# Moving masking and weight scaling between GpSimd and ScalarE in a top-k attention and channel-mixing kernel

## The chip, the cores and the metric

The kernel runs on one core of a Trainium2 chip. The metric is the time of one execution on the device in microseconds, as the median of several runs. The core has five engines that run side by side, each through its own list of instructions in order: TensorE (PE) for matrix products, VectorE (DVE), ScalarE (ACT), GpSimd (POOL) and SyncE (SP), which here only issues DMA transfers. They wait for each other through semaphores.

## The reference

Inputs are q, k and v of shape (8 batches, 8 heads, 576 rows, 64), float32, and the parameters U (576 x 32), V (32 x 576), w_ch1 (512 x 2048) and w_ch2 (2048 x 512). These four are float64, since they are float32 arrays multiplied by a float64 scalar. The kernel sees them as pairs of 32-bit words, low and high.

```python
scores = scale * np.matmul(q, k.transpose(0, 1, 3, 2))
kth = np.partition(scores, -32, axis=-1)[..., -32:-31]
scores = np.where(scores >= kth, scores, -1e9)
attn = softmax(scores)                    # over the last axis
x = concat_heads(np.matmul(attn, v))      # (8, 576, 512)
u = x + (x.T @ U @ V).T                   # per batch
out = u + np.maximum(u @ w_ch1, 0.0) @ w_ch2
```

So each row of 576 scores keeps its 32 largest values. The rest get no weight.

## The kernel before, in words

**Tiles and steps.** The work goes by head pairs g (32 of them, four per batch) and, within a pair, by row tiles t: four of 128 rows for both heads, and a tail t = 4 in which the 64 last rows of both heads share one tile. A list of steps holds them in order. In the first batch (g below 4) each tile is a step, 20 in all; later the tail shares the step of t = 3, so that a pair has four steps. The main loop goes over steps n and writes out by hand, per step, in which order the engines get their instructions. Because each engine works in order, that text order is the schedule.

**Finding the 32nd largest.** `front` is a generator, advanced by `next(here)` and `next(last)` at chosen places of a step. For each lane (one head's 128 x 576 scores) DVE finds the eight largest (L507, MAX8), replaces them by a very small number (L520) and finds the next eight (L525), four rounds in all. From the second batch on (`blocked`), scores are folded first: the larger of each two (L434) and the sum less the larger (L432, L435 on POOL) make halves that the rounds then search (L486, L488).

**Masking and weighing.** `ways` says how a lane is masked. A "gap" lane: ACT scales the 32nd value (L551), writes to E how far each score lies below it, times a huge factor (L554), and POOL subtracts that from the scores (L555, two operands). A "pooled" lane: POOL compares and multiplies (L530, one operand and a value per partition) and adds the outcome (L531, two operands). An "early" lane is masked on DVE (L534). In the first batch lane 1 is pooled and lane 0 a gap, apart from the last tile and the last tail of the batch; later all are gaps. Then ACT takes the exponential and its sum (`weigh`, L439). The gap lanes of step n - 1 are masked at the start of step n (`next(last)`), the pooled ones at the end of their own step.

**Turning and multiplying.** PE turns the weights (L617, L622), ACT copies them out (L618, L623), and PE multiplies by v (`values`, L691, L694). From pair 6 on DVE turns them in blocks (L581) with a trip through DRAM instead. `mixed` builds u for a batch, and `mlp` makes its two big products (L816, L834), which `fill` scatters over later steps as filler for PE. `mlp` of batch b can begin only when the attention of batch b is done. The last batch uses another product scheme (`closing`, L910).

**The parameters.** 36 pieces, most of them 128 x 512, are turned from float64 words to float32. One call of `next_params(1)` does three things in this order. It finishes the waiting ACT passes and joins the piece that was split at the call before (`f64_join`: a shift on DVE, L188, and two additions on POOL, L189 and L191). It splits the piece that was loaded at the call before (`f64_parts`: it queues three ACT passes, L176 scaling the high words into the destination, L177 from a byte of the low words, L180 the sign of the high words, written in place). It issues the load of a new piece (L154, SP, three buffers). `fill` also pops one queued pass each time. In the first batch a step has a call after the first round for t = 0, 1, 2 and one after the third for t = 0, 1, 3. In the second batch the calls stand before `fill` after the first round (not for g = 4, t = 3) and near the end of the step, after loads and turned keys.

**The start.** For the first pair `prep` turns queries on PE and copies them with ACT (L321, L323), then the 64 last rows of both (L313, L316), then the keys, copied by DVE. `scores` makes two PSUM tiles. For the first tile DVE copies the first one (L390) and ACT the second in two instructions (L391, L392).

The passages that the steps of the prediction lean on most:

```python
for c, chunk, *_ in gaps:
    gap = attn.tile([P, S], F32, tag="E", name="E")
    nc.scalar.activation(gap, chunk, AF.Relu, bias=least[:, c : c + 1], scale=-WIDEN)
    nc.gpsimd.tensor_tensor(chunk, chunk, gap, ALU.subtract)
```

Of the kernel before, what the change touches and what calls it, by code (L numbers as in the profile page):

```python
# [8 lines left out]
F32 = mybir.dt.float32  # L9
U8 = mybir.dt.uint8  # L10
U32 = mybir.dt.uint32
AF = mybir.ActivationFunctionType
# [14 lines left out]
def kernel(  # L27
# [94 lines left out]

    nudge = const.tile([P, 1], F32, name="nudge")
    nc.vector.memset(nudge, TINY)
    eps = const.tile([P, 1], F32, name="eps")
    nc.vector.memset(eps, 1e-9)

# [10 lines left out]
        return slice(h * D, (h + 1) * D)  # L138

    SLAB = 512  # L140
    spare = []


# [13 lines left out]
    def f64_parts(raw, out):  # L157

        n, w = raw.shape[0], raw.shape[-1] // 2
        d = "p f" if len(raw.shape) == 3 else "p"
        low, hi = (raw.rearrange(f"{d} (w two) -> {d} w two", two=2)[..., i] for i in range(2))
        low8 = raw.bitcast(U8).rearrange(f"{d} (w eight) -> {d} w eight", eight=8)[..., 3]
        if out is None:
            if not spare:

                uT = mlpp.tile([P, NC, S], F32, tag="uT", name="uT")
                words = uT.rearrange("p c n -> p (c n)").bitcast(U32)  # L170
                spare.extend(words[:, i * SLAB : (i + 1) * SLAB] for i in range(NT))
            out = spare.pop()[0:n, 0:w]
        bits = out.bitcast(U32)
        lows, his = low.bitcast(F32), hi.bitcast(F32)
        passes.extend((
            lambda: nc.scalar.activation(bits.bitcast(F32), his, AF.Copy, scale=RESCALE),  # L176
            lambda: nc.scalar.activation(  # L177
                lows, low8, AF.Identity, bias=four[0:n], scale=-(1 + 2.0**-10) * 2.0**-26
            ),
            lambda: nc.scalar.activation(his, his, AF.Sign, bias=nudge[0:n]),  # L180
        ))
        return hi, bits, low
# [118 lines left out]
    def prep(g):  # L301

        qkT = attn.tile([P, 2, S], F32, tag="qkT", name="qkT")
        qkTs[g] = qkT
        if blocked(g):
            nc.vector.transpose(qkT.rearrange("p i n -> p (i n)"), raw.pop(g))
            yield
            return
        tiles, ends = raw.pop(g)
        for i in (0, 2, 1) if g == 0 else (0, 1, 2):  # L310
            if i == 2:
                tp = ps_t.tile([P, 2, TAIL], F32, tag="tp", name="tp")
                nc.tensor.transpose(  # L313
                    tp.rearrange("p i n -> p (i n)"), ends.rearrange("p h d -> p (h d)"), ident
                )
                nc.scalar.copy(qkT[:, :, MAIN:S], tp)  # L316
                yield
                continue
            tp = ps_t.tile([P, NT, P], F32, tag="tp", name="tp")
            for c in range(NT):  # L320
                nc.tensor.transpose(tp[:, c, :], tiles[i][:, c].rearrange("p h d -> p (h d)"), ident)  # L321
            copy = nc.vector.tensor_copy if g == 0 and i else nc.scalar.copy
            copy(qkT[:, i, 0:MAIN], tp.rearrange("p t n -> p (t n)"))  # L323
            yield

    def scores(g, t, tail=False):
# [61 lines left out]
        last = S2[:, MAIN : MAIN + 2 * TAIL].rearrange("p (h n) -> p h n", h=2)  # L388
        copy = nc.vector.tensor_copy if g + t == 0 else nc.scalar.copy
        copy(main[:, :, 0:HALF], scs[0][:, :, 0:HALF])  # L390
        nc.scalar.copy(main[:, :, HALF:MAIN], scs[1][:, :, 0 : MAIN - HALF])  # L391
        nc.scalar.copy(last, scs[1][:, :, MAIN - HALF : HALF])  # L392
        if tail:
            tail_copies(g, scs, third)

# [45 lines left out]
    def ways(g, t):  # L441

        if (g, t) == (NPAIR - 1, NT - 1):
            return (0,), (), (1,)
        if (g, t) == (NPAIR - 1, NT):
            return (0,), (), ()
        if t == NT:
            return (), (), (0,)
        return ((), (1,), (0,)) if g < NPAIR else ((), (), (1, 0))

    def eased(g, t):
        return bool(ways(g, t)[2])

    def front(tiles):

# [4 lines left out]
        for g, t in tiles:  # L460
            if t == 0:
                dens[g] = small.tile([P, 2 * NT + 1], F32, tag="den", name="den", bufs=3)
            S2, den = S2s.pop((g, t)), dens[g]
            early, pooled, gaps = ways(g, t)
            n = S2.shape[1]
            fold_of = folds.pop((g, t), None)
            for c in (1, 0) if n == 2 else (0,):
                slot = c if n == 2 or len(tiles) == 1 else 2
                spot = CH * c + t if g >= NPAIR else 2 * t + c
                lanes.append((  # L470
                    slot,
                    S2[:, c],
                    den[:, spot : spot + 1],
                    [a[:, c] for a in fold_of] if fold_of else None,
                    "early" if c in early else "pooled" if c in pooled else "gap" if c in gaps else "",
                ))
        W = len(lanes)
        first = small.tile([P, 3, 8], F32, tag="first", name="first", bufs=3)
# [30 lines left out]
        for i in range(1, TOPK // 8):  # L509
            if i == 1:  # L510
                nc.scalar.mul(nmax[:, 0:W], first[:, 0:W, 0], -SCALE)
                Es = {}
                for c, chunk, _, _, way in lanes:
                    if way == "early":
                        Es[c] = attn.tile([P, S], F32, tag="E", name="E")
                        weigh(chunk, Es[c], nmax[:, c : c + 1])
            for c in order:

                nxt = places.pop(c, curs[c])
                nc.vector.match_replace(nxt, ms[c], curs[c], NEG)  # L520
                curs[c] = nxt
            m8 = small.tile([P, 3, 8], F32, tag="m8", name="m8", bufs=4)
            for c in order:
                ms[c] = m8[:, c]
                nc.vector.max(ms[c], curs[c])  # L525
            yield
        for c, chunk, total, _, way in lanes:
            if way == "pooled":
                gap = attn.tile([P, S], F32, tag="E", name="E")
                nc.gpsimd.tensor_scalar(gap, chunk, ms[c][:, 7:8], NEG, ALU.is_lt, ALU.mult)  # L530
                nc.gpsimd.tensor_tensor(chunk, chunk, gap, ALU.add)  # L531
        for c, chunk, total, _, way in lanes:
            if way == "early":
                nc.vector.scalar_tensor_tensor(  # L534
# [23 lines left out]
        if len(gaps) > 1:  # L558
            c, chunk, total, *_ = rest.pop(0)
            weigh(chunk, chunk, nmax[:, c : c + 1], total)  # L560
            yield
        for c, chunk, total, *_ in rest:
            weigh(chunk, chunk, nmax[:, c : c + 1], total)
        if t == NT and g != NPAIR - 1:
# [623 lines left out]
    for n in range(STEPS + 2):  # L1188
# [89 lines left out]
        for tile_ in tiles(n + 1):  # L1278
            if tile_[1] < NT:
                scores(*tile_, len(tiles(n + 1)) > 1)  # L1280
            fold(*tile_)
        turn()
        fill()
        turn()
# [7 lines left out]
        if n < STEPS and n - 2 >= ALONE and len(tiles(n - 2)) > 1:  # L1292
            scale(steps[n - 2][0][0])
        next(here, None)
        border = g == NPAIR and t == NT - 1
        if not border:
            next_params(1)
        fill()
        if n >= STEPS:
            if n == STEPS:  # L1300
# [3 lines left out]
        next(here, None)  # L1304
        for tile_ in tiles(n + 1):
            split(*tile_)
        fill()
        next(here, None)
        for tile_ in tiles(n - 1):
# [7 lines left out]
                coming = loading(g + 2) if g + 2 < NP else iter(())  # L1317
            next(coming, None)
        next(ready, None)
        if t != 0 or g == NPAIR + 1:  # L1320
            next_params(1)
        next(here, None)
        fill()
        fill()
# [35 lines left out]
```

## Time and profile before

| What | us |
|---|---|
| Median of 3 runs (1663.66 to 1663.92) | 1663.71 |
| The profiled execution's own time | 1662.32 |
| Its span | 1660.2 |
| Busy: PE, DVE, ACT, POOL | 1555.9, 1547.4, 995.1, 1009.4 |
| L555 on POOL, 243 times, mean | 1.419 |
| L530 on POOL, 15 times, mean in 20 to 230 us | 2.222 |
| L188 on DVE at 128 x 512, shortest, median, longest up to 340 us | 0.380, 0.408, 1.378 |

The profile is of one execution. A line of a timeline gives the start and the length in us, the engine, the line of the code, the operation, what is written from what, and in brackets the idle time of the engine before it and what ended it. In the slices, the span is cut into 40 equal parts (41.5 us each) and a digit gives the busy tenths of a part. The chain of waits follows the work back from the end: each piece of time goes to the instruction that the next one had to wait for. PE's ends are modelled, so a busy PE need not be at its peak.

### The profile page before, as it was taken

Reading aid. Unit: us, or ns where it says so; the run is one execution under the profiler, and the core shown is the slowest. Engines: PE = TensorE matmul, PEld = TensorE weight load, DVE = VectorE, ACT = ScalarE, POOL = GpSimd, SP = SyncE. Lnnn points to the kernel's source line nnn. Section 1 sums busy time; section 2 is a strip of 40 time slices with the busy share of each in tenths; the row PEclk is TensorE's granted clock in tenths of the full one; section 3 lists DMA queues with packets and bytes.
Section 4 is the critical chain, followed back from the end, with each engine's and each line's share of the span. In section 5 each row is a group of like instructions: output and inputs, shape, how many; then the busy total and the mean of one; then the engine's idle time right before and its main releaser. Section 6 shows DMA issues by size and latency. Waiting matters only on the chain.

```text
span 1660.2 us, 30248 instructions
## 1 busy us (share of the span) xinstructions
PE 1555.9 (94%) x9638; PEld 1183.2 (71%) x9638; DVE 1547.4 (93%) x4393; ACT 995.1 (60%) x2475; POOL 1009.4 (61%) x881
## 2 busy tenths in 40 slices
PE   4566698999899999999999999999999999999999
PEld 2444466777677887778777887778777887777776
DVE  7999998999999999999999999999999999994452
ACT  4888778665655666566665666565665656563320
POOL 4787669766656565656656565666666566663620
PEclk7777899999999999999999999999999999999999
DMA  3323223255555555554555565555555555543001
GB/s 88 90 83 92 69 83 86 63 128 133 131 131 130 140 148 138 127 142 130 130 128 137 133 154 133 131 139 133 139 122 142 127 146 135 141 126 97 10 1 29
DMA packets 280399, 189.42 MB, mean 114 GB/s; under 512 B 174288, under 2 KB 261168, under 8 KB 280240
## 3 DMA queue, kind: packets, MB, share of 16 engines
q1 hardware_dynamic: 259728, 117.62, 30.9%
q10 hardware_dynamic: 20512, 69.87, 13.6%
q8 instruction: 76, 1.25, 0.3%
q14 instruction: 83, 0.68, 0.1%
HBM read 116.49 MB, written 70.91 MB: 113 GB/s over the span
## 4 chain that ended last, share of the span: by engine, by line
PE 66%; DVE 25%; DMA 4%; SPq 1%; issue 1%; ACT 1%; POOL 1%; DVEq 0%; ACTq 0%; POOLq 0%
PE mm L834 21%; PE mm L816 19%; DVE m L525 8%; DVE upper L520 7%; PE sc L336 6%; PE O L694 5%; PE mm L910 3%; DVE first L507 3%; PE tp L910 2%; PE sc L910 2%; PE sc L368 2%; DMA PT<-away 2%; PE up L766 1%; DVE y L581 1%; DVE upper L488 1%; DVE place L520 1%
## 5 line engine op out<-in xcount | busy, mean ns | idle before, releaser
L834 PE MATMUL mm<-hT,w 128*128 128x320 f32 (+1 forms) x1792 | 462.1, 407 | 0.0
L816 PE MATMUL mm<-uT,w 128*128 128x320 f32 (+1 forms) x1792 | 459.8, 409 | 1.2 <-ACT hT L829 1.0
L555 POOL TENSOR_TENSOR Ssb<-Ssb,E 128x576 f32<-128x576 f32 x243 | 340.0, 1419 | 185.4 <-ACT E L554 185.2
L816 PEld LDWEIGHTS mm<-uT,w 128*128 128x128 f32 x1792 | 334.1, 190 | 100.7 <-issue 10.6
L834 PEld LDWEIGHTS mm<-hT,w 128*128 128x128 f32 x1792 | 332.0, 190 | 93.0 <-issue 10.2
L525 DVE MAX8 m<-upper 128x8 f32<-128x304 f32 (+1 forms) x774 | 362.5, 509 | 0.7
L520 DVE MATCH_REPLACE8 upper<-m,upper 128x304 f32<-128x304 f32 (+1 forms) x516 | 256.6, 504 | 0.0
L435 POOL TENSOR_TENSOR lower<-lower,upper 128x576 uint32<-128x576 uint32 x108 | 152.5, 1412 | 141.7 <-DVE upper L434 137.2
L432 POOL TENSOR_TENSOR lower<-Ssb 128x576 uint32<-128x576 uint32 x108 | 152.4, 1411 | 116.3 <-ACT Ssb L381 65.9
L439 ACT ACTIVATE Ssb<-Ssb,nmax 128x576 f32<-128x576 f32 x258 | 201.8, 784 | 28.8 <-POOL Ssb L531 10.3
L336 PE MATMUL sc<-qkT 64*128 64x288 f32 (+1 forms) x1056 | 176.9, 457 | 9.1 <-ACT Ssb L390 8.2
L554 ACT ACTIVATE E<-Ssb,least 128x576 f32<-128x576 f32 x243 | 176.3, 769 | 4.2
L488 DVE MAX8 upper<-lower 128x8 f32<-128x288 f32 x432 | 171.8, 438 | 2.3 <-POOL lower L435 2.3
L381 ACT COPY Ssb<-sc 128x576 f32<-128x576 f32 x216 | 127.7, 643 | 66.8 <-PE sc L336 66.3
L829 ACT ACTIVATE hT<-mm 128x320 f32<-128x320 f32 (+1 forms) x224 | 91.9, 411 | 107.3 <-PE mm L816 102.2
L581 DVE STREAM_TRANSPOSE y<-Ssb 128x512 f32<-128x512 f32 (+1 forms) x312 | 153.9, 544 | 0.0
L694 PE MATMUL O<-PT,va 128*64 128x128 f32 x2048 | 144.0, 284 | 0.0
L336 PEld LDWEIGHTS sc<-qkT 64*128 64x128 f32 (+1 forms) x1056 | 95.2, 196 | 49.2 <-issue 17.0
L694 PEld LDWEIGHTS O<-PT,va 128*64 128x64 f32 x2048 | 112.7, 140 | 16.2 <-issue 1.6
L520 DVE MATCH_REPLACE8 upper<-first,upper 128x304 f32<-128x304 f32 x216 | 97.5, 458 | 0.0
L486 DVE MATCH_REPLACE8 lower<-upper,lower 128x288 f32<-128x288 f32 x216 | 93.9, 442 | 0.0
L507 DVE MAX8 first<-upper 128x8 f32<-128x304 f32 x216 | 90.1, 458 | 0.0
(266 smaller groups left out, 2208.4 us busy)
## 6 DMA issues: line engine op xcount, KB each, us to landing
away<-y SPq DMA_DIRECT2D x416, 144.0 KB
PT<-away ACTq DMA_DIRECT2D x104, 576.0 KB
raw<-in_moe_w_ch_dram SPq DMA_DIRECT2D x32, 512.0 KB
va<-in_v_dram SPq DMA_DIRECT2D x64, 128.0 KB
scale<-rd ACTq DMA_DIRECT2D x56, 144.0 KB
out_dram<-ob SPq DMA_DIRECT2D x59, 128.0 KB
ld<-in_q_dram SPq DMA_DIRECT2D x108, 64.0 KB
ld<-in_k_dram SPq DMA_DIRECT2D x108, 64.0 KB
```

Of the source, the lines that this page charges most:

```text
L336: nc.tensor.matmul(out, lhsT=qkT[half(h), 0, cols(t)], rhs=qkT[half(h), 1, lo:hi], start=True, stop=True,)
L435: nc.gpsimd.tensor_tensor(bottom, bottom, top.bitcast(U32), ALU.subtract)
L439: nc.scalar.activation(E, chunk, AF.Exp, bias=nmax, scale=SCALE, accum_out=total)
L488: nc.vector.max(spot, lower)
L520: nc.vector.match_replace(nxt, ms[c], curs[c], NEG)
L525: nc.vector.max(ms[c], curs[c])
L554: nc.scalar.activation(gap, chunk, AF.Relu, bias=least[:, c : c + 1], scale=-WIDEN)
L555: nc.gpsimd.tensor_tensor(chunk, chunk, gap, ALU.subtract)
L581: nc.vector.transpose(y[:, :, i * NT : i * NT + c].rearrange("p r c j -> p c r j"), E2[:, a : a + c * P].rearrange("p (c r j) -> p c r j", ...
L694: nc.tensor.matmul(O[half(h)], lhsT=va[:, h, j, :], rhs=PT[:, NT * h + j], start=False, stop=(j == NT - 1),)
L816: nc.tensor.matmul(ph[:, 0:w], lhsT=first_layer(cc, f), rhs=uT[:, cc, lo:hi], start=(cc == 0), stop=(cc == NC - 1),)
L834: nc.tensor.matmul(po[:, 0:w], lhsT=w2[:, f, c * P : (c + 1) * P], rhs=hTs[f][:, 0:w], start=(f == 0), stop=(f == NF - 1),)
```

## The change

It makes these edits:

- In the first batch both lanes of a tile are gap lanes; the pooled way is gone (L530 and L531 are no longer there, L551 now covers two lanes). The extra `yield` between the two weighings stays for later batches only. The ring of m8 has 7 buffers in place of 4.
- The scaling of a parameter piece (L176 on ACT) is a POOL multiplication by a broadcast constant while at least 12 pieces are still to be loaded, that is for the first 24. It is issued at once in `f64_parts`, not queued as a pass.
- In the second batch the first call of a step stands right after the scores of the next tile, and the second after the split, for t = 0, 1, 2. Step 23 (g = 4, t = 3) joins a piece at its first call.
- The first pair's keys are turned before the last rows. For the very first tile ACT copies the second PSUM tile's main part head by head, head 1 first, and DVE the two last strips.

PE's list of instructions is otherwise the same, in the same order.

```diff
@@ f64_parts
+        if len(params) >= LATE:          # LATE = 12
+            factor = rescale[0:n] if len(raw.shape) == 2 else rescale[0:n].rearrange("p o -> p o ()")
+            nc.gpsimd.tensor_tensor(
+                bits.bitcast(F32), his, factor.to_broadcast(list(bits.shape)), ALU.mult
+            )
+        else:
+            passes.append(
+                lambda: nc.scalar.activation(bits.bitcast(F32), his, AF.Copy, scale=RESCALE)
+            )
         passes.extend((
-            lambda: nc.scalar.activation(bits.bitcast(F32), his, AF.Copy, scale=RESCALE),
@@ prep
-        for i in (0, 2, 1) if g == 0 else (0, 1, 2):
+        for i in range(3):
@@ scores
-        nc.scalar.copy(main[:, :, HALF:MAIN], scs[1][:, :, 0 : MAIN - HALF])
-        nc.scalar.copy(last, scs[1][:, :, MAIN - HALF : HALF])
+        for h in ((1,), (0,)) if g + t == 0 else ((0, 1),):
+            hs = slice(h[0], h[-1] + 1)
+            nc.scalar.copy(main[:, hs, HALF:MAIN], scs[1][:, hs, 0 : MAIN - HALF])
+        copy(last, scs[1][:, :, MAIN - HALF : HALF])
@@ ways
-        return ((), (1,), (0,)) if g < NPAIR else ((), (), (1, 0))
+        return (), (1, 0)
@@ front
-            m8 = small.tile([P, 3, 8], F32, tag="m8", name="m8", bufs=4)
+            m8 = small.tile([P, 3, 8], F32, tag="m8", name="m8", bufs=7)
-        for c, chunk, total, _, way in lanes:
-            if way == "pooled":
-                gap = attn.tile([P, S], F32, tag="E", name="E")
-                nc.gpsimd.tensor_scalar(gap, chunk, ms[c][:, 7:8], NEG, ALU.is_lt, ALU.mult)
-                nc.gpsimd.tensor_tensor(chunk, chunk, gap, ALU.add)
             weigh(chunk, chunk, nmax[:, c : c + 1], total)
-            yield
+            if g >= NPAIR:
+                yield
@@ main loop, second batch on
             fold(*tile_)
+        next_params(1)
         turn()
...
         next(here, None)
-        border = g == NPAIR and t == NT - 1
-        if not border:
-            next_params(1)
         fill()
...
             split(*tile_)
+        if t < NT - 1:
+            next_params(1)
         fill()
...
         next(ready, None)
-        if t != 0 or g == NPAIR + 1:
-            next_params(1)
         next(here, None)
```

More of the change, by code (lines that the diff above doesn't have):

```diff
@@ L124 @@
     nc.vector.memset(nudge, TINY)
+    rescale = const.tile([P, 1], F32, name="rescale")
+    nc.vector.memset(rescale, RESCALE)
     eps = const.tile([P, 1], F32, name="eps")
@@ L140 @@
     SLAB = 512
+    LATE = 12
     spare = []
@@ L443, in ways @@
         if (g, t) == (NPAIR - 1, NT - 1):
-            return (0,), (), (1,)
+            return (0,), (1,)
         if (g, t) == (NPAIR - 1, NT):
-            return (0,), (), ()
+            return (0,), ()
         if t == NT:
-            return (), (), (0,)
-        return ((), (1,), (0,)) if g < NPAIR else ((), (), (1, 0))
+            return (), (0,)
+        return (), (1, 0)
     def eased(g, t):
-        return bool(ways(g, t)[2])
+        return bool(ways(g, t)[1])
     def front(tiles):
@@ L463, in front @@
             S2, den = S2s.pop((g, t)), dens[g]
-            early, pooled, gaps = ways(g, t)
+            early, gaps = ways(g, t)
             n = S2.shape[1]
@@ L474, in front @@
                     [a[:, c] for a in fold_of] if fold_of else None,
-                    "early" if c in early else "pooled" if c in pooled else "gap" if c in gaps else "",
+                    "early" if c in early else "gap" if c in gaps else "",
                 ))
```

## The prediction

> **What bounds the kernel now.** I read the slices of the span first, then the chain of waits, then the timelines of DVE, POOL, ACT and PE over the first 340 us, since everything that the change touches lies there.
>
> ```profile
> DVE  7999998999999999999999999999999999994452
> ACT  4888778665655666566665666565665656563320
> POOL 4787669766656565656656565666666566663620
> ...
> PE 66%; DVE 25%; DMA 4%; SPq 1%; issue 1%; ACT 1%; POOL 1%; DVEq 0%; ACTq 0%; POOLq 0%
> ```
>
> ```profile
> 170.23 1.29 POOL L191 TENSOR_TENSOR w<-w,raw 128x512 uint32<-128x512 uint32 x1
> ...
> 174.57 2.26 POOL L530 TENSOR_SCALAR E<-Ssb,m 128x576 f32<-128x576 f32 x1
> ```
>
> ```profile
> 165.09 0.41 DVE L188 TENSOR_SCALAR w<-w 128x512 uint32<-128x512 uint32 x1
> ...
> 170.97 0.84 DVE L188 TENSOR_SCALAR w<-w 128x512 uint32<-128x512 uint32 x1
> ...
> 175.91 0.40 DVE L188 TENSOR_SCALAR w<-w 128x512 uint32<-128x512 uint32 x1
> ```
>
> DVE is busy nine tenths or more in nearly every slice up to 1490 us. From 11.3 to 257.9 us it has no idle worth naming, so in the first batch the time is the sum of DVE's own instructions, and ACT and POOL count only where they make DVE stand. PE has idle time until about 266 us, hardly any in 266 to 327, some in 400 to 448, and none worth naming afterwards up to the end: after 448 us it works through a fixed list. So what DVE gains or loses in the first batch is passed on whole, and what is gained after 266 us is passed on only as far as PE moves too.
>
> The three L188 lines carry most of what follows. L188 takes 0.40 us alone. At 170.97 it took 0.84, because POOL's two-operand L191 ran until 171.52; it ended 0.29 later. At 175.91 it took 0.40 in the middle of POOL's one-operand L530. Who starts first matters: at 154.73 POOL's L555 began, L188 0.05 us later passed in 0.41, and that L555 took 1.72 for its usual 1.41; at 203.53 L188 came 0.21 after L739 and took 1.12.
>
> [...]
>
> **Part by part.** The sum is made against the profiled execution, 1662.32 us (span 1660.2, so 2.1 around it); the median shown is 1.39 above it.
>
> *Engine loads, first batch.* POOL loses 15 L530 of 2.22 and 15 L531 of 1.41 (54.4 us) and gains 15 L555 of 1.41 (21.2) and 24 scalings. No row shows the scaling. From below: L739, also a float multiply by a broadcast operand at 512 elements, 1.04; from above by its shape: L189, which reads the same stride, 1.29; from far above L530, 2.22 at 576, so 1.97 at 512. I take 1.04, the nearest. ACT loses 24 L176 (0.67 at 512) and gains 15 L554 (0.77). Both are off the path in this batch: ACT works 32 to 33 of 40 us there, POOL 30 to 33. What counts is where POOL's two-operand instructions now fall against L188.
>
> [...]
>
> *Start: -1.05.* Now the keys' transposes stand behind those of the last rows, which wait for a load until 6.07; the keys' copy begins at 7.44. Turned first, they can begin when the queries' end, at about 5.5, so the copy comes 0.75 earlier. Then ACT's 0.53 and 0.27 (L391, L392, 10.52 to 11.22) become one copy of 224 columns, an estimated 0.36 between these two, beside DVE's 128 columns: 0.3 less before the first L507 (11.26). The load of the keys is issued before that of the last rows; if it landed only with it, the gain is 0.3. From -0.3 to -1.2.
>
> *L188 in the first batch: +4.6.* Steps 0 and 1 of a head pair have two parameter calls, step 2 has one at its middle. Take L188 of the second call, ending at 0. POOL follows with L189 (starts at 0.08, next after 1.37), L191 (1.26) and now the scaling (1.00 from start to start, as L739 to L189), so the two L555 of the step start at 3.71; ACT has written their E by then (L551 plus twice 0.70 after the last MAX8). The next L188 comes at 4.02, 0.31 after the first L555 (from 160.66 + 0.41 to 165.09). Today L530 runs there and costs nothing. L555 holds it until 5.11 + 0.28, so it takes 1.37 in place of 0.41: +0.96, twice per pair, in pairs 1 to 3: +5.8. The 0.43 that the second call of step 1 costs now (77.46, 124.20, 170.97) goes, since POOL is done 0.5 us before: -1.3. In pair 0 the 0.82 at 25.14 for a 32-wide L188 goes (-0.7), while the one at 35.86 must wait 0.3 for the scaling behind the four L191 and then meets L555 within 0.1 us: 0.3 to 1.7, taken as 0.8. Sum +4.6; if L188 wins all its meetings, -1.4.
>
> *Steps 20 to 23: +0.3.* The calls stand earlier in their steps, so one more L188 (0.33) falls before 247.9. Against POOL's rows the stalls of the moved ones are about 0.2, 0.25, 0 and 0 to 0.3 and 0.4, and the 0.62 at 214.22 goes. POOL's queue gets no longer.
>
> *Second batch: -3.6.* The last MAX8 of step 23 ends at 247.87; then L188 0.40, L189 1.29, L191 1.28, and only then L555, so ACT's third mask waits until 252.32:
>
> ```profile
> 248.28 1.30 POOL w L189
> 249.57 0.07 issue
> 249.64 1.28 POOL w L191
> 250.93 1.37 POOL Ssb L555
> 252.30 0.02 issue
> 252.32 0.78 ACT E L554
> ```
>
> With that pair done before, L555 begins with its mask (248.95) and ACT goes on at 250.35: -1.97. An L180 less stands ahead of L703, so PE's transposes start not at 254.27 (after 6.18 idle) but about 2.6 earlier; two more PE waits for L703 and L554 (1.29 at 266.32, 0.49 at 305.45) shrink. That makes 3.6 on PE. DVE would gain more: its idle of 2.18, 0.20, 1.69 and 1.31 before 287 and 4.6 us of L188 stalls from 252.82 to 294.11, of which I keep about half, since L188 still meets L555 or L191. But scores come in PE's order, which the change leaves alone here; DVE already waits 1.86 at 329.07 for scores and will wait longer. So PE's 3.6 is the term; from 0 (PE waits elsewhere) to -5.5.
>
> *At nothing:* SP's raw loads move ahead of the key and query loads. Key loads issued at 262 to 268 are read by L306 at 283.39, 15 us of cover; without it L306 and so DVE would stand for the transfer, 4.6 us in the chain. The added DVE memset runs before 5 us, where DVE is idle. A new wait: L180 overwrites what the scaling reads, so ACT can stand behind POOL with L551, L554 and the score copies queued after it. The scaling ends at 8.3 us of a two-call step, L180 is due there, and the copies that DVE needs are a step ahead.
>
> Sum: -1.05 + 4.6 + 0.3 - 3.6 = +0.25; 1662.6 for the profiled execution, and with the 1.39, **1664.0**.
>
> **Rivals.** *L188 wins its meetings.* If the scaling costs 1.26 from start to start (L189's row), L555 starts at 3.97, 0.05 before L188, which is the gap at 154.73 where L188 passed. Then the L188 term is -1.4 in place of +4.6: sum -5.75, time 1658.0. For it: the strided read of L189. Against: L739's 1.04.
>
> *POOL becomes the gate (slower).* If the scaling costs what L530's row gives, 1.97, POOL's work in a two-call step is 2 x 2.63 + 2 x 1.97 + 2.75 = 11.9 us against DVE's 10.3. L188 then waits for the scaling itself: by the same offsets 0.7, 1.7 and 0.8 per pair, +3.2 less 0.43, three times, +8.3, with 0.6 in pair 0: sum +4.6 to 1668.3; where L555 also slips in first, six times 1.4 more, 1676.7. It decides from 1.47 us per scaling, where the second call of step 1 begins to wait. Against it: no two-operand row of 512 elements is above 1.31 unless it was held up.
>
> *The second batch's gain does not arrive*, because ACT, with the same six passes per step, is late at another place: +3.85, 1667.6.
>
> *The change does nothing*: if L188 falls beside L555 half the time and PE moves by 1: near 1663.
>
> **How the numbers follow.** The sum near nothing, with the small rival: 0.45, 1661 to 1667. L188 passes: 0.28, 1658. POOL the gate: 0.17, 1668 to 1677. No gain in the second batch: 0.10. Range 1656 to 1671: it takes in the bounds of start, second batch and most of the slow rival. About 0.2% (3.3 us) can be told from no change: faster by more 0.31, within 0.42, slower by more 0.27.
>
> **What would show it.** First L507 at about 10.2. The scaling group's mean, 1.04 or 1.29. L188 of 1.3 to 1.4 at the first call of steps 1 and 2 in each pair, and 0.41 at the second call of step 1. The step 23 MAX8 some 4 us later than 247.87; DVE's wait for ACT before L634 gone; PE's idle at the tail of step 23 down from 6.2 to about 4. I am wrong if DVE idles on POOL in the first batch, or if PE stands again between 266 and 400 us.

## The result and the profile after

| | Median, us | Ratio to the kernel before, with its 95% interval |
|---|---|---|
| Kernel before, in the runs beside the first measurement (8 runs, 1662.5 to 1664.72) | 1663.68 | 1 |
| Changed kernel, first measurement (8 runs, 1666.66 to 1671.12) | 1668.78 | 1.0032 [1.0022, 1.0043] |
| Changed kernel, second measurement (9 runs, 1665.88 to 1670.46) | 1666.89 | 1.0021 [1.0011, 1.0031] |

The changed kernel is slower by 0.2 to 0.3%. The time lies in the range forecast; the forecast itself was no change, and the sum behind it is 3.4 to 4.9 us too low. The changed kernel's own runs also spread over 4.5 us in each measurement, against 2.2 of the kernel before beside the first (8 runs) and 3.5 beside the second (19 runs). The profiled execution of the first measurement was its slowest: 1671.12 us, with a span of 1669.2.

Lines of the changed kernel are shifted: the shift on DVE is L199 (was L188), the two additions on POOL L200 and L202 (L189, L191), the new scaling on POOL L180, ACT's scaling L185 (L176), the sign L191 (L180), the gap mask L562 on ACT and L563 on POOL (L554, L555), the weighing L452 (L439), the score copies L401, L404, L405 (L390 to L392), the first MAX8 L520 (L507). In the experiments the lines move by a few more; the operation and the tiles name them.

The slices and the shares of the chain of waits, after:

```profile
DVE  7999999999999999999999999999999999994452
ACT  4777787665565656556565666566665656563320
POOL 3676668766565666666656565656666566663620
...
PE 47%; DVE 37%; DMA 7%; SPq 4%; POOL 2%; ACT 2%; issue 2%; DVEq 0%; ACTq 0%; POOLq 0%
```

Over the whole span nothing much has moved: DVE is as full as before. The chain's split between PE and DVE (66 and 25 before) should not be read as a cause. Where two engines are equally late it can follow either: the kernel with the start's edits alone, whose time does not differ, has 56 and 30. The difference must be looked for in the first 340 us, and there by landmarks that every kernel has: A, the first MAX8; B, the shift ahead of step 19's first MAX8 (191.43 before); C, the first MAX8 of step 24 (250.43 before; an expectation below calls it step 23's mark); E, the MAX8 that stood at 323.09 before.

| Profile | A | A to B | B to C | C to E | E to the end |
|---|---|---|---|---|---|
| before | 11.26 | 180.17 | 59.00 | 72.66 | 1337.1 |
| after, first | 11.14 | 185.46 | 63.17 | 70.09 | 1339.3 |
| after, second (e5) | 10.66 | 185.42 | 61.25 | 70.14 | 1337.7 |
| p1 start alone | 11.25 | 180.19 | 58.40 | 72.73 | 1338.9 |
| p2 mask alone | 11.34 | 178.43 | 59.33 | 72.67 | 1337.9 |
| p3 scaling alone | 11.19 | 190.36 | 59.88 | 72.48 | 1337.0 |
| p4 places alone | 11.28 | 180.15 | 59.99 | 70.20 | 1339.4 |
| e6 after without scaling | 10.74 | 178.20 | 58.95 | 70.13 | 1337.3 |
| e7 half the scaling | 10.81 | 183.23 | 60.46 | 70.11 | 1337.2 |
| e8 long scaling | 11.27 | 187.81 | 60.26 | 70.12 | 1338.2 |
| e9 more scaling | 10.90 | 191.64 | 61.78 | 70.09 | 1338.9 |
| e10 busy PE | 11.23 | 185.52 | 62.17 | 70.12 | 1336.8 |
| e11 one less | 11.14 | 185.43 | 58.93 | 70.11 | 1338.9 |
| e12 five less | 11.02 | 183.48 | 60.29 | 70.07 | 1338.8 |

So the changed kernel loses 5.3 us in the first batch and 2.2 to 4.2 at the border of the batches, and wins 2.5 in the second batch and at most 0.6 at the start. Every later row is read against this table.

In the first batch the loss is the one that the prediction drew. The timeline of POOL and DVE in the changed kernel, pair 3:

```profile
167.44 1.05 POOL L180 TENSOR_TENSOR w<-raw,rescale 128x512 f32<-128x512 f32 x1
168.45 2.98 POOL L563 TENSOR_TENSOR Ssb<-Ssb,E 128x576 f32<-128x576 f32 x2
...
168.72 1.43 DVE L199 TENSOR_SCALAR w<-w 128x512 uint32<-128x512 uint32 x1
```

The scaling takes 1.05. The first of the two masks behind it begins 0.27 ahead of the shift, and the shift takes 1.43 for its usual 0.40. In pairs 1 to 3 this happens six times, at 72.26, 83.66, 120.50, 131.90, 168.72 and 180.13, with 1.34 to 1.43 each; the second call of step 1 takes 0.40 to 0.41 where it took 0.82 to 0.85.

At the border there is something that the prediction did not have. The waits of DVE from 200 to 340 us, after (summed, times, longest):

```profile
DVE upper L501 <- POOL lower L448: 2.7, 2, 1.8
DVE first L520 <- ACT Ssb L405: 2.6, 1, 2.6
DVE upper L447 <- ACT Stail L414: 2.1, 1, 2.1
DVE upright L643 <- ACT den L574: 0.8, 1, 0.8
DVE w L199 <- ACT w L185: 0.6, 1, 0.6
```

DVE stands 2.6 for the scores of step 21 (L405) and 0.6 for ACT's scaling right after; neither wait was there before. The wait for ACT ahead of L643, once 2.2, is down to 0.8 (the forecast had it gone), but 2.7 for the folded halves on POOL (L448) took much of its place; up to the same point it was 1.3 before.

### The profile page after: what moved, and what is told of

Same layout as the page of the kernel before. It is cut to its first block, busy times and chain, and to the rows that moved or that the text cites. A ratio compares the mean times of both kernels' runs of the same rounds, so it can differ in the third digit from the quotient of the medians.

```text
span 1669.2 us, 30225 instructions
## 1 busy us (share of the span) xinstructions
PE 1561.5 (94%) x9638; PEld 1188.0 (71%) x9638; DVE 1553.5 (93%) x4395; ACT 992.0 (59%) x2466; POOL 998.3 (60%) x890
## 3 DMA queue, kind: packets, MB, share of 16 engines
q8 instruction: 76, 1.25, 0.3%
## 4 chain that ended last, share of the span: by engine, by line
PE 47%; DVE 37%; DMA 7%; SPq 4%; POOL 2%; ACT 2%; issue 2%; DVEq 0%; ACTq 0%; POOLq 0%
PE mm L843 14%; PE mm L825 12%; DVE m L538 10%; DVE upper L533 9%; PE sc L347 4%; DVE y L590 4%; PE O L703 4%; DVE first L520 3%; DVE upper L501 3%; PE mm L919 3%; DVE place L533 2%; DMA PT<-away 2%; PE tp L919 2%; PE sc L919 2%; DMA ld<-in_k_dram 2%
## 5 line engine op out<-in xcount | busy, mean ns | idle before, releaser
L563 POOL TENSOR_TENSOR Ssb<-Ssb,E 128x576 f32<-128x576 f32 x258 | 360.8, 1420 | 207.3 <-ACT E L562 207.1
L448 POOL TENSOR_TENSOR lower<-lower,upper 128x576 uint32<-128x576 uint32 x108 | 152.3, 1410 | 137.2 <-DVE upper L447 135.2
L452 ACT ACTIVATE Ssb<-Ssb,nmax 128x576 f32<-128x576 f32 x258 | 201.9, 784 | 17.5 <-DMA away<-y 6.2
L562 ACT ACTIVATE E<-Ssb,least 128x576 f32<-128x576 f32 x258 | 186.2, 768 | 4.2
L392 ACT COPY Ssb<-sc 128x576 f32<-128x576 f32 x216 | 127.6, 644 | 66.5 <-PE sc L347 66.1
L520 DVE MAX8 first<-upper 128x8 f32<-128x304 f32 x216 | 90.3, 459 | 0.0
```

Source lines behind the costliest of these rows:

```text
L452: nc.scalar.activation(E, chunk, AF.Exp, bias=nmax, scale=SCALE, accum_out=total)
```

## The experiments

The theory after this profile: the scaling on POOL pushes the masks onto the shift (A to B), a stretch of half clock on PE costs the wait at step 21, and start, mask and places cost nothing. The rivals: the mask by gaps itself, or the earlier calls of the second batch, or ACT waiting for POOL's scaling.

**The four parts one by one.** Each is the kernel before with one part of the diff shown above.

The start alone:

```diff
-        for i in (0, 2, 1) if g == 0 else (0, 1, 2):
+        for i in range(3):
...
+        copy(last, scs[1][:, :, MAIN - HALF : HALF])
```

> The kernel before with the start's edits alone: keys turned ahead of the last rows, and DVE's copy of the two last strips of the first scores. The profile of the changed kernel shows its first MAX8 at 11.14 us against 11.26, with the keys' copy 0.74 earlier. Theory: the time won at the keys is lost again before the scores, since the last rows' transposes now stand between keys and scores on PE and DVE's copy of the strips stands behind two copies of ACT; first MAX8 at 11.1 to 11.2, time 0.1 us less than before, not to be told from it. Rival: the start alone gives the 1.05 us that I forecast, and in the changed kernel another part took it back; first MAX8 near 10.2, 1662.6 against 1663.7.

Measured: 1663.18 against 1663.44, ratio 1.0000 [0.9991, 1.0009]. DVE's timeline at the start of this kernel:

```profile
6.81 0.69 DVE L323 COPY qkT<-tp 128x512 f32<-128x512 f32 x1 [5.86 <-PE tp L321]
9.34 0.76 DVE L390 COPY Ssb<-sc 128x576 f32<-128x576 f32 x1 [1.84 <-PE sc L336]
10.93 0.29 DVE L394 COPY Ssb<-sc 128x128 f32<-128x128 f32 x1 [0.83 <-ACT Ssb L393]
```

The keys' copy comes 0.63 earlier than the 7.44 of before, but from there to the first MAX8 it is 4.44 us where it was 3.82. The scores now wait for the last rows as well (1.84 ahead of L390 in place of 1.43), and DVE's strips wait 0.83 for ACT's second copy before they take 0.29 (before, the first MAX8 itself waited 0.93 for ACT). What was won is spent on the way. In kernels with this start A lay between 10.66 and 11.27, as the keys' load let PE begin earlier or later: at 5.33 in e9, 5.58 in the changed kernel's first profile and 5.67 in e10, with A at 10.90, 11.14 and 11.23.

The mask by gaps alone:

```diff
-        return ((), (1,), (0,)) if g < NPAIR else ((), (), (1, 0))
+        return (), (), (1, 0)
...
-            yield
+            if g >= NPAIR:
+                yield
```

The ring of m8 has its 7 buffers here too.

> The kernel before with one edit: the first batch's mask of chunk 1 is made by the gap form (ACT's L554 and POOL's L555) in place of POOL's L530 and L531. The scaling stays on ACT. Theory: the 5.2 us that the changed kernel lost between 11 and 197 us come from the scaling, which pushes POOL's L555 to where DVE's shift of the next parameter stands; without it L555 starts 1.0 us earlier, L188 passes as it ends, and the 0.82 to 0.85 at the second call of step 1 goes as well: a landmark at 191.43 comes 0 to 1.5 us earlier, time 1662 to 1664. Rival 1: the gap form by itself does it (L188 beside L555 wherever they meet, or ACT's extra pass makes the scores late): 191.43 comes 4 to 5 us later, time 1667 to 1669. Rival 2: no scaling on POOL and 54 us of POOL work less frees DVE by more than 2 us: below 1661.5.

Measured: 1660.82, ratio 0.9985 [0.9976, 0.9994], 2.6 us less; A to B is 1.74 shorter. The gap form by itself costs nothing: rival 1 falls, and the gain is a little over the theory's 0 to 1.5. By its time the run meets rival 2's mark (below 1661.5); by A to B, where that rival asked for more than 2 us, it does not. Some 1.3 of the 1.74 are the three long shifts at the second call of step 1, which are gone: all shifts of pairs 1 to 3 take 0.40 to 0.58. What the rest of the time comes from is not shown.

The scaling alone (`LATE = 12`, the diff of `f64_parts`):

> The kernel before with one edit: 24 scalings of parameters on POOL in place of ACT; the first batch keeps POOL's L530 and L531. Theory: POOL's work in a step with two calls is then 2 x (1.37 + 1.28 + 1.04) for the parameters, 2.22 + 1.41 for the mask and 1.41 for the gap, 12.4 us against DVE's 10.3, so POOL becomes the gate there, steps with one call win some back, and L188 waits for the scaling itself: 6 to 12 us more in the first batch, time 1669 to 1676. Rival: ACT's 24 passes less (16 us) free the score copies, POOL's backlog is taken up in the third step of each pair, and L188 stands only beside two-operand instructions: 0 to 3 us more, 1663.5 to 1667.

Measured: 1672.62, ratio 1.0055 [1.0041, 1.0069], 9.2 us more, and A to B 10.2 longer. DVE's waits from 11 to 200 us:

```profile
DVE w L199 <- POOL w L180: 8.0, 3, 2.9
```

Three waits of 2.1 to 2.9, once per pair from pair 1 on, at the second call of step 1: here POOL is the gate, as the prediction's slower rival describes it. In the changed kernel it isn't, since the gap form has no L530 (2.22).

The places alone:

```diff
+        next_params(1)
         turn()
...
-        border = g == NPAIR and t == NT - 1
-        if not border:
-            next_params(1)
...
+        if t < NT - 1:
+            next_params(1)
...
-        if t != 0 or g == NPAIR + 1:
-            next_params(1)
```

> The kernel before with one edit: the second batch's parameter calls at other places of a step (a call ahead of step 20's turn, none after the second turn of steps 21 to 23). First batch, start and scaling as before. In the changed kernel the keys of the last pair were ready 9.3 us later than before, of which 5.2 had come from the first batch and some 2.6 to 3.2 stood at step 21 beside a half clock of PE; 2.1 us came back later. Theory: those 2.6 to 3.2 us are not the places' doing, so that the places alone cost some 1 us up to 231 us and give back 2 to 3.6 later: time 1661 to 1663. Rival: the earlier call puts parameter work of ACT and POOL ahead of step 21's scores, and that made them late: DVE idles 2 to 3 us behind ACT near 210 us here too, with PE's clock at 1.0 there, time 1664 to 1666.

Measured: 1662.09, ratio 0.9991 [0.9983, 1.0000], 1.35 less, as the theory had it. C to E is 2.46 shorter, as in every kernel with these places. DVE does not wait for step 21's scores here; its one wait near 210 us is 0.47, for ACT's scaling. The rival falls.

The four differences add up to +4.9, near the 5.1 of the first measurement. That should not be taken for additivity: mask, start and places without the scaling gave more than their sum, as the next group shows.

**How much scaling.** The next four are the changed kernel with one edit or none.

> The changed kernel once more, for a second profile. The single edits gave -0.3 (start), -2.6 (mask by gaps), +9.2 (scaling on POOL) and -1.4 (places); their sum is +4.9, and the change as a whole cost 5.1. In the first profile of the changed kernel PE's clock was 0.50 from 205 to 215 us, and DVE idled 2.63 and 0.59 at step 21; that run, 1671.1, was the slowest of eight (median 1668.8). Theory: these 3.2 us belong to where the half-clock window happened to fall, not to the edit: in a profile in which PE has full clock between 205 and 215, the idle at step 21 is under 0.6, and the run's time is 1666 to 1669; the stalls of the shift (1.3 to 1.4, six of them in pairs 1 to 3) stand in both profiles. Rival: the parameters' work on ACT and POOL ahead of step 21 makes its scores late whatever the clock: the idle of 2.6 is there again with the clock at 1.0.

Measured: 1666.89, ratio 1.0021 [1.0011, 1.0031]. The six long shifts stand here too (1.34 to 1.43). At step 21 DVE idles 0.70 in place of 2.63, which is more than the 0.6 I had allowed, with less half clock; the 0.59 behind it is the same in both. PE's granted clock (the third figure from the right), first in the first profile, then in this one:

```profile
205.00:210.00 5.00, 4.37 (x27) 3.41 (x27) 4.96 (x13) 1.71 (x5) 0.00 (x0) 0.51 0.38 59
210.00:215.00 5.00, 4.57 (x25) 3.38 (x23) 5.00 (x11) 2.19 (x6) 1.04 (x1) 0.50 0.00 0
```

```profile
205.00:210.00 5.00, 4.25 (x27) 3.31 (x26) 4.96 (x14) 2.15 (x5) 0.00 (x0) 0.66 0.37 58
210.00:215.00 5.00, 4.30 (x32) 2.83 (x33) 4.48 (x9) 2.79 (x9) 1.04 (x1) 1.00 0.00 0
```

Cut into halves of a microsecond, the stretch at 0.50 lasts from 205.2 to 215.4 in the first and from 205.9 to 209.3 in the second: 10.2 and 3.4 us for one and the same program. So the 1.9 us between the two in B to C (63.17 against 61.25) come from the execution, not from the program.

Without the scaling on POOL (`LATE = 100`):

> The changed kernel with the scaling left on ACT: start, mask by gaps and places remain. Theory: the scaling on POOL is the only part that costs, and the others add up: -0.3 - 2.6 - 1.4 = -4.3 against the kernel before, 1658.5 to 1660.5, and no shift in the first batch above 0.6 us. Rival: the mask's gain and the places' gain are the same gain (both bring the border forward to a PE that then stands in the way), so that only the larger arrives: 1660.5 to 1662.

Measured: 1657.44, ratio 0.9965 [0.9952, 0.9977], 5.8 less than the kernel before and 9.4 less than the changed one beside it. DVE has no wait from 11 to 195 us. The third rival, ACT waiting for POOL's scaling, does not explain the first batch either: in the changed kernel ACT's sign passes wait 18.7 us in all for that scaling from 11 to 200 us, but from 12 us on DVE stands only 0.2 us there. POOL and DVE at the place shown above:

```profile
160.51 1.28 POOL L202 TENSOR_TENSOR w<-w,raw 128x512 uint32<-128x512 uint32 x1
161.75 2.98 POOL L563 TENSOR_TENSOR Ssb<-Ssb,E 128x576 f32<-128x576 f32 x2
163.04 0.41 DVE L199 TENSOR_SCALAR w<-w 128x512 uint32<-128x512 uint32 x1
```

The mask follows the addition directly, so its first half has only 0.1 us to go when the shift starts. The shift passes in its usual 0.41, and the second half takes 1.61, held up in its turn. The rival (one gain counted twice) falls. The outcome is even 1.6 better than the sum of the parts; the table puts 0.5 of it at A, and p4 lost some at a border with a stretch of half clock (201.1 to 204.5). The rest I have not traced.

Half of each scaling on POOL, half on ACT:

```diff
+            to, k = bits.bitcast(F32), w // 2
+            nc.gpsimd.tensor_tensor(to[..., 0:k], his[..., 0:k], factor..., ALU.mult)
+            passes.append(lambda: nc.scalar.activation(to[..., k:w], his[..., k:w], AF.Copy, scale=RESCALE))
```

> The changed kernel with half of each scaling's columns on POOL (256 of 512) and the other half on ACT. It doses the delay. Theory: POOL's L555 starts 0.5 us earlier than in the changed kernel (two-operand work of some 0.52 in place of 1.04), so it ends some 0.5 after the next shift of DVE starts in place of 1.0: the six long shifts of pairs 1 to 3 take 0.8 to 1.0 us in place of 1.35 to 1.43, 2.5 to 3 us less than the changed kernel, 1665 to 1667. Rival: DVE is held by any scaling on POOL that is queued ahead of the mask (the count of POOL's instructions or ACT's sign pass waiting for them counts, not when L555 ends): the six stay at 1.3 to 1.4, 1668 to 1670.

Measured: 1664.79, ratio 1.0007 [0.9999, 1.0016], 2.1 less than the changed kernel. The same place:

```profile
118.29 0.61 POOL L181 TENSOR_TENSOR w<-raw,rescale 128x256 f32<-128x256 f32 x1
118.86 2.96 POOL L567 TENSOR_TENSOR Ssb<-Ssb,E 128x576 f32<-128x576 f32 x2
119.57 0.98 DVE L203 TENSOR_SCALAR w<-w 128x512 uint32<-128x512 uint32 x1
```

The scaling is 0.44 shorter, and the shift takes 0.98 in place of 1.43; the six take 0.91 to 1.00, as the theory said. The time is 0.2 below the theory's range. The dose decides, not whether there is a scaling.

The factor read from a full tile:

```diff
-    rescale = const.tile([P, 1], F32, name="rescale")
+    rescale = const.tile([P, P], F32, name="rescale")
...
+            factor = rescale[0:n, 0:e].rearrange("p e -> p () e")
```

> The changed kernel with the scaling's factor read from a full tile in four groups of 128 in place of one value; meant to make POOL's scaling longer, near the 1.29 of a row that reads the same stride and a full second operand. Theory (it counts who starts first): with 1.25 or more per scaling L555 starts after DVE's shift has started, the shift passes in 0.41, and L555 takes 1.6 to 1.7: 4 to 6 us less than the changed kernel although POOL works more, 1662.5 to 1665. Rival: more work on POOL is more delay: the shifts stay at 1.35 or grow, and DVE idles on POOL at the second call of step 1; 1669 to 1674. If the scaling stays at 1.04 the run tells nothing and the time is that of the changed kernel.

Measured: 1671.28, ratio 1.0044 [1.0031, 1.0056]. The scaling took 1.30, as intended, and the theory failed: the shifts grew to 1.60 to 1.63.

```profile
120.40 1.30 POOL L183 TENSOR_TENSOR w<-raw,rescale 128x512 f32<-128x512 f32 x1
121.67 1.40 POOL L564 TENSOR_TENSOR Ssb<-Ssb,E 128x576 f32<-128x576 f32 x1
121.74 1.62 DVE L200 TENSOR_SCALAR w<-w 128x512 uint32<-128x512 uint32 x1
```

I took the 0.07 for a near miss and made the next kernel to pass it.

**Who starts first.** More work on POOL ahead of the mask:

```diff
+            for k in (w * 3 // 8, w):
+                nc.gpsimd.tensor_tensor(to[..., 0:k], his[..., 0:k], factor..., ALU.mult)
```

> The changed kernel with more work for POOL: each scaling is preceded by one of its first 192 columns of 512, which writes the same values, by the half scaling's 0.61 and the whole one's 1.04 some 0.5 us. In the run with the long scaling (1.29) L555's counterpart still began 0.07 us ahead of DVE's shift (121.67 against 121.74), and the shift waited it out whole: 1.62, ended 0.28 after it. So that run did not reach the condition it was made for. Here POOL's mask would begin 0.4 to 0.5 later than in the changed kernel, 0.1 to 0.2 after the shift has begun. Theory (who starts first counts): the six shifts take 0.40 to 0.45, the mask behind each takes 1.6 to 1.75 for its usual 1.4, and the first batch is 5 to 6 us shorter than the changed kernel's: 1660.5 to 1663 against 1666.9, by doing more on POOL. Rival (POOL's load counts): the shift waits as before or longer, and DVE idles on POOL at the second call of step 1: 1669 or more.

Measured: 1673.78, ratio 1.0069 [1.0056, 1.0081]; the theory fell again.

```profile
121.89 1.63 POOL L182 TENSOR_TENSOR w<-raw,rescale 128x192 f32<-128x192 f32 x2
123.47 1.41 POOL L565 TENSOR_TENSOR Ssb<-Ssb,E 128x576 f32<-128x576 f32 x1
123.55 1.62 DVE L201 TENSOR_SCALAR w<-w 128x512 uint32<-128x512 uint32 x1 [0.59 <-POOL w L182]
```

The bracket tells why there is no such race to win. The shift works on the very piece that this scaling writes, so it waits for the scaling, and when it is released (0.08 after the mask's start) POOL has already gone on to the next instruction of its own list, the mask. A longer scaling did not let the shift pass at any of the six places; it added its own wait (0.31 to 0.59) to the full 1.60 to 1.63. In e8 each of the six starts 0.03 to 0.04 after the scaling's end and 0.07 to 0.09 after the mask's start, as in e9 (0.07 to 0.08), so lengthening the scaling does not move the two against each other.

PE kept busier, to hold its clock:

```diff
+                for _ in range(3 if g in (2, 3) else 1):
                     product(sc[:, h, 0:HALF], h, part * HALF, (part + 1) * HALF)
```

> The changed kernel with each score product of pairs 2 and 3 made three times over, which writes the same values and gives PE some 2.5 us more work per step between about 90 and 200 us, where it has idle time. Theory: the half clock of PE in the first batch follows its idle time; with PE busier the clock stays at 1.0 from about 110 to 257 us, the wait for scores at step 21 (2.63 in one profile, 0.70 in the other) falls under 0.3, and the time is 0 to 1.5 us below the 1666.9 of the changed kernel and spreads less. Rival: the windows come whatever PE does, or the clock falls from more work; then the extra products at half clock (5 us per step) delay the score copies, DVE idles on them in the first batch, and the time is 3 us or more above the changed kernel's.

Measured: 1668.37, ratio 1.0034 [1.0024, 1.0044], not to be told from the changed kernel. PE's work between 100 and 200 us was 79.0 us at a mean clock of 0.86, against 61.2 at 0.83 and 65.5 at 0.78 in the changed kernel's two profiles. Half clock still came there and from 206.0 to 212.8, and DVE idled 1.64 at step 21. A to B is as in the changed kernel, so the extra products cost nothing. Neither the theory nor the rival holds as stated. If more work raised the clock, it was by little, and it did not keep it up across the border, where PE waits for ACT (1.9 us at the longest). What would keep it up stays open.

**The last scaling.** `LATE = 13`: the last of the 24 scalings goes back to ACT.

> The changed kernel with one scaling fewer on POOL, the last of 24 (LATE = 13). From the shift at the start of step 19 to step 23's mark (191.43 to 250.43 before, 59.00) the places alone took 59.99, mask, places and start without the scaling 58.95, the changed kernel 61.25 in its second profile and 63.17 in its first, the one with ten us of half clock. In both profiles of the changed kernel the last scaling (199.68) stands on POOL ahead of the mask that ACT's L452 waits for (1.33), and the copies of step 20's scores and the copy that PE's next transposes need are queued behind that L452, 0.6 us later against their step than without the scaling. Theory: this one scaling causes 1 to 1.5 us of the border's loss: 59.7 to 60.3 in its profile, if PE's clock is not lower than in the second profile, no wait of DVE for the scores at step 21 over 0.3, and a time 1 to 1.5 below 1666.9. Rival: the loss at the border comes from the whole first batch's backlog on POOL and ACT, or from the clock: 61 or more, the wait at step 21 stays at 0.7 or above.

Measured: 1666.40, ratio 1.0019 [1.0010, 1.0028]. By time this is inconclusive: 3.0 over its runs of before, where the changed kernel had 3.6 and 5.1. The profile is clearer. POOL and ACT around 200 us, first in the changed kernel's first profile, then here:

```profile
200.21 1.04 POOL L180 TENSOR_TENSOR w<-raw,rescale 128x512 f32<-128x512 f32 x1
...
201.21 1.41 POOL L563 TENSOR_TENSOR Ssb<-Ssb,E 128x576 f32<-128x576 f32 x1
202.65 0.78 ACT L452 ACTIVATE Ssb<-Ssb,nmax 128x576 f32<-128x576 f32 x1 [1.33 <-POOL Ssb L563]
...
203.43 0.62 ACT L401 COPY Ssb<-sc 128x576 f32<-128x576 f32 x1
```

```profile
200.17 1.41 POOL L563 TENSOR_TENSOR Ssb<-Ssb,E 128x576 f32<-128x576 f32 x1
...
201.62 0.78 ACT L452 ACTIVATE Ssb<-Ssb,nmax 128x576 f32<-128x576 f32 x1 [0.41 <-POOL Ssb L563]
...
202.39 0.62 ACT L401 COPY Ssb<-sc 128x576 f32<-128x576 f32 x1
```

ACT's weighing waits 1.33 for the mask behind the scaling, 0.41 without it, and the score copies queued behind it come 1.0 earlier. In e11 DVE has no wait at all from 192 to 255 us, and B to C is 58.93, even less than expected. But its clock was 1.0 from 200 to 215, so this profile alone does not part the two causes. Two others help. e8 has the scaling, and the clock is 1.0 over the same stretch; e12, shown next, has no scaling at this place, but one stretch of half clock (203.4 to 206.8, so part of both its rows here). The clock is again the third figure from the right, first in e8, then in e12:

```profile
205.00:210.00 5.00, 3.88 (x39) 2.85 (x39) 4.40 (x14) 3.85 (x10) 0.40 (x1) 1.00 0.53 111
```

```profile
200.00:205.00 5.00, 2.71 (x19) 2.06 (x19) 4.90 (x14) 2.96 (x9) 0.00 (x0) 0.83 0.61 140
205.00:210.00 5.00, 4.44 (x37) 3.29 (x33) 5.00 (x12) 2.68 (x7) 1.04 (x1) 0.83 0.19 30
```

| B to C | Full clock at the border | One stretch of 3.4 us at half clock |
|---|---|---|
| Without the last scaling on POOL | 58.93 (e11), 58.95 (e6) | 60.29 (e12) |
| With it | 60.26 (e8) | 61.25 (e5) |

With the scaling and 6.8 us at half clock it is 62.17 (e10), with 10.2 us 63.17 (the first profile). So the last scaling goes with 1.0 to 1.3 us, and each 3.4 us at half clock with 0.9 to 1.4. These are single profiles, and e12 lacks four more scalings before this one. The kernel before and p1, alike in this part and both at full clock there, differ by 0.6 (59.00 and 58.40). In e8 all scalings are longer, so ACT comes late to the border anyway: it does not wait for the mask there, and DVE's one wait is 0.48, for the weighing.

`LATE = 17`: the five scalings of the batch's last pair go back to ACT.

> The changed kernel with five scalings fewer on POOL (LATE = 17): the last pair of the first batch has its parameters scaled by ACT. Theory: besides what one scaling fewer gives (1 to 1.5), the two long shifts of that pair (1.43 and 1.34) go back to 0.41, 1.9 us, and the other long ones stay: 1663 to 1664.5, and the run of long shifts ends at about 132 us. Rival: the stalls of pairs 1 to 3 hang together through POOL's backlog, so that the last pair's shifts stay above 1 us: 1665 to 1667.

Measured: 1664.12, ratio 1.0008 [0.9999, 1.0017], as the theory said. The two shifts of pair 3 that were long are 0.42 and 0.40, those of pairs 1 and 2 stay at 1.34 to 1.43, and A to B is 1.94 shorter than in the changed kernel. The stalls do not hang together; each is paid for where it stands.

## Why the prediction was right in part

- **The mechanism in the first batch was right.** Six shifts beside L555 at +0.96 each were forecast, and 1.34 to 1.43 measured for 0.41, so +0.93 to +1.02; the 0.43 at the second call of step 1 went, as forecast. The term was +4.6 and measured 5.25 to 5.3. The difference lies in pair 0: +0.88 by the first MAX8 of step 3, where I had +0.1 (the 64-wide shift took 1.39 and waited 0.23 for the scaling).
- **The scaling's price was right**: 1.04 to 1.05. The slower rival (POOL the gate) did not come in the changed kernel; p3 shows its mechanism with the old mask. A longer scaling made the first batch's term larger: with 0.61 (e7), 1.04 to 1.05 and 1.30 (e8) the six shifts took 0.91 to 1.00, 1.34 to 1.43 and 1.60 to 1.63.
- **The largest rival could not happen.** I gave 0.28 to the shift passing first, if the scaling were longer. e8 and e9 show that the shift waits for that scaling, behind which the mask already stands. The dependence can be read in the code: `f64_join` shifts the piece that `f64_parts` scaled at the call before. (Its -1.4 would also be -1.7 by its own terms: -1.3, -0.7 and +0.3.)
- **The step that failed is "Steps 20 to 23: +0.3"**, with its sentence that POOL's queue gets no longer. There the changed kernel's profiles lost 2.25 and 4.17. The places themselves took nothing: at full clock e6 has 58.95 for B to C, the kernel before with the old places 59.00. What I missed is the one scaling of the border that stands ahead of the tail's mask. I had asked only what stands behind POOL's scaling on DVE, and had written that ACT's copies are a step ahead; at the border ACT waits for that mask with step 20's score copies behind it. By the profiles of the section above this goes with 1.0 to 1.3 us; by time e11 gained only 0.5 on the changed kernel. The half clock on PE came on top. What sets its stretches there stays open.
- **The second batch's term was mis-sized**: -3.6, measured -2.5 in every kernel with these places. The wait for ACT went from 2.2 to 0.8 and the one of 1.7 for ACT's scaling went altogether, and PE's idle before L626 (L617) fell from 6.18 to 4.03, where I had about 4; but 1.4 more of waits for POOL's fold came in place of what DVE won, and its seven shifts still cost 6.7 us in place of 7.5.
- **The start was mis-sized**: -1.05, measured 0 in time (p1) and -0.6 to 0 at A. The keys' gain was right (0.61 to 1.22 earlier, for 0.75); what I left out is that the last rows' transposes then stand between keys and scores, and that DVE's strips wait for ACT.

By these terms the second profile gives -0.60 + 5.25 + 2.25 - 2.52 = +4.4, and +0.6 after E: 5.0, the difference of the spans. All four terms missed to the same side, so nothing cancelled. That the time still lies in the range is partly luck. The second batch's miss lies within the bounds that the range allowed for, but the border's loss is in no bound of it; the range's upper part was there for the slow rival, which did not come. A time slower by more than 0.2% had been given a chance of 0.27.

## What to carry to other kernels

The scaling went to an engine with idle time (POOL was busy 73.3 of the 100 us from 100 to 200) and still delayed what was queued behind it there: shifts of 1.34 to 1.43 in place of 0.41, and 1.33 of ACT's waiting at the border in place of 0.41. So ask of each moved instruction who waits for its successor, and ask it again at the border of two stages, where the others have no lead. Where an instruction waited for another engine and then competed with that engine's next instruction, it started second, by 0.07 to 0.09 us in e8 and 0.07 to 0.08 in e9, so making the first one longer did not help. Of the four parts, three together (mask, start, places) are worth 0.35% [0.23, 0.48], and the fourth takes more than that back.

## What the runs showed of the hardware

- In the first 345 us of the 14 profiles there are 166 places where a two-operand POOL instruction had begun 0.07 to 1.05 us ahead of a 128 x 512 shift on DVE. The shift ended 0.28 to 0.29 after that instruction at every one, for example started 0.07, 0.27 or 0.71 into it (1.62, 1.43, 0.98). The first of a merged pair of masks is taken as 1.41 here, as where it stands alone. So at each of these places the shift was held to the end of POOL's instruction.
- At all ten places where POOL had begun at most 0.06 ahead, the shift passed in 0.40 to 0.41, and the POOL instruction took 1.68 to 1.74 for its usual 1.41. In the kernel before:

```profile
154.73 1.72 POOL L555 TENSOR_TENSOR Ssb<-Ssb,E 128x576 f32<-128x576 f32 x1 [1.88 <-ACT E L554]
154.78 0.41 DVE L188 TENSOR_SCALAR w<-w 128x512 uint32<-128x512 uint32 x1
```

- A one-operand POOL instruction did not always let the shift pass either. In p3, where it had begun 0.06 ahead six times, the shift took 0.43 four times and 0.96 twice; begun 1.25 to 1.34 ahead, as in the kernel before, it never held the shift (0.40 to 0.41).
- On POOL a multiplication by one broadcast value took 1.04 at 512 columns and 0.61 at 256; with the factor read from a full tile it took 1.30 at 512.
- At the border PE's clock fell to half for 3.4 us (from 205.9) and for 10.2 us (from 205.2) in two executions of one program; DVE's wait at step 21 was 0.70 and 2.63 in these two. In e10 it fell to half for 6.8 us (from 206.0), and the wait was 1.64.
